# One bank for the small results of logits, routing and slots, the experts' order copied by VectorE, and one conversion step moved

## The chip, the core and the metric

The kernel runs on one core of a Trainium2 chip. The metric is the device time of one execution in microseconds (us), median of three runs. The core has five engines with an instruction queue each, which run in order: TensorE (PE; its weight loads are shown as PEld), VectorE (DVE), ScalarE (ACT), GpSimd (POOL) and SyncE (SP), which only issues transfers here. PE writes its results to PSUM, eight banks of 512 float32 columns in 128 partitions.

## What is computed

Two batches of 768 tokens pass through three layers: attention over a window with a few global keys, a mixture of experts with one expert for each token, and a mixing layer.

```python
scores = q @ k.T / 8 - slopes * dist          # 8 heads of 64, window of 96, 8 global keys
attn = softmax(where(keep, scores, -1e9)) @ v
logits = x @ w_gate                           # 8 experts
local = sigmoid(x @ w_local)
e[s] = argmax(logits[s]) if s == 0 or local[s] < 0.5 else e[s - 1]
out[s] = softmax(logits[s])[e] * (relu(x[s] @ w1[e]) @ w2[e])
theta = out @ w_theta
y = w_tok_r @ (out * cos(theta)) + w_tok_i @ (out * sin(theta))
u = out + y
result = u + relu(u @ w_ch)
```

## The kernel before

The order of all instructions is written out by hand; the framework adds the waits on semaphores. The work falls into attention with routing, the experts and the mixing layer. This change lies in the first of them and in its passage to the second.

**The attention loop.** There are 12 blocks of 128 tokens, each with 4 units (a unit is two heads). The loop over `s` has 24 steps of two units each, so a block takes an even and an odd step. Names of the pieces of work, as the list `TAIL` and the calls of `at` use them:

- `qk` scores on PE (L557); `sa`, `sb` the softmax of the two heads: a subtraction of the minimum on DVE (L579) and the exponential on ACT (L589).
- `tr` transposes the probabilities of a unit on PE into a tile `pt` (L612); `cp` copies it out, on ACT (L621) or, for every fourth unit, on DVE (L619); `pv` multiplies with the values (L636).
- For a block `i`: `ev` copies the result out (ACT, L648), `ri` takes the reciprocals (DVE, L602 and L603), `yt` transposes it on PE (L653) into a `pt` buffer, `ys` scales and stores it (DVE, L662; for the last two blocks ACT and POOL).
- The block's logits: `lg` on PE (L219), `lc` copies them on ACT (L223), `lt` transposes them on PE (L226), `ld` divides and sums on DVE (L231 writes `lh`, L237).
- Routing of a pair `t` of blocks: `ch` (DVE, L252 to L260), `ro` (PE, L266 and L267), `sc` (DVE, L272 and L274), `oh` (PE, L285), `ho` (DVE, L290), `po` (PE, L301 and L302), `pl` (DVE, L307 to L313), `mk` (POOL or DVE, L321), `sl` (PE, L330), `tk` (DVE, L341 and L343).
- `ha`, `hb`, `hr`, `ya`, `yb`, `px`, `pc`: an expert's first 128 tokens, computed ahead, on PE and ACT.
- `rk`, `en`: the experts' ranking and `experts_slots` on DVE. `le`, `lx`, `ls`: the choice of the expert that is computed ahead.
- `job_tick` (and `jt`): the next of six stages that convert a 512-column piece of a later layer's weights, on ACT and DVE; the fifth also issues the load of a later piece, the sixth is a subtraction on DVE (L414). `JATT` lists the steps that end with such a stage.

In the odd steps that end a pair, with X = 4t + 9, the order is `qk`, `oh`, `lc`, `lt`, `ys`, then the softmax of the first unit, `ho`, `ld`, then `tr`, `tr`. In the steps X = 4t + 11 `lc`, `lt`, `ys`, `ld`, `ch` come in the same places and `sl` ends the step. In the even steps `ro` or `po` follow `qk`, and `yt`, `lg` end the step.

**PSUM.** The pool `pT` has two buffers of one bank, tag `pt`, taken in turn. They hold the transposed probabilities, the transposed blocks (`yt`), the logits and the slots. The pool `pM` has one bank, tag `m`, which holds the routing's small results (`misc`) and the warm-up's. The choice between the two:

```python
def mps(own):
    return (pM if own else pT).tile([128, 512], F32, tag="m" if own else "pt", name="m")
```

**The passage to the experts.** SP loads the weights in pieces. The first load of `w1` needs `first_i` only; every later one needs `order_g`, a copy of `order_i` that POOL makes behind three gathers of tokens (L1029, L1040). The first piece's `w2` (L1017), the next pieces and all that follow stand behind that.

Of the kernel before, what the change touches and what calls it, by code (L numbers as in the profile page):

```python
# [9 lines left out]
F32 = mybir.dt.float32  # L10
F32R = mybir.dt.float32r
BF16 = mybir.dt.bfloat16
I32 = mybir.dt.int32
AF = mybir.ActivationFunctionType
# [42 lines left out]

TAIL = """
ev10 ro4 tk3 tr46 tr47 sc4 cp46 oh4 ho4 cp47 pv44 pv45 yt10 lg10 ri10 lc10 po4 pl4 px pc lt10 ys10 ld10 pv46 pv47 ev11
ri11 mk4 ha0 hb0 hr0 jt yt11 lg11 lc11 jt ha1 hb1 hr1 lt11 ld11 ys11 sl4 tk4 ya0 yb0 ch5 ha2 hb2 hr2 ro5 sc5 ya1 yb1 oh5  # L60
jt ho5 ha3 hb3 hr3 po5 pl5 ya2 yb2 mk5 rk ha4 hb4 hr4 sl5 tk5 ya3 yb3 ha5 hb5 hr5 en ya4 yb4 ha6 hb6 hr6 ya5 yb5 ha7 hb7
hr7 ya6 yb6 ya7 yb7 ye
"""
# [4 lines left out]
CPV0 = (1, 3)  # L68


JATT = (4, 5, 6, 8, 9, 10, 12, 13, 14, 16, 17, 18, 20, 21, 22)
JRATE = (0.8, 1.4, 1.3, 1.9, 2.5, 2.5, 1.6)
T1, T2, T3 = 2, 2, 2
JBUFS = 3
# [26 lines left out]
def kernel(  # L101
# [13 lines left out]
    V, A, G, PE, SP = nc.vector, nc.scalar, nc.gpsimd, nc.tensor, nc.sync  # L115
# [6 lines left out]
    def ct(shape, dt, name):  # L122
        return const.tile(shape, dt, name=name, tag=name)
# [9 lines left out]
    wg = ct([128, 4, 32], F32, "wg")  # L133


    ident = ct([128, 128], F32, "ident")
# [73 lines left out]
    def logit_stages(blk, xT, rinv, ps, sb):  # L210

        st = {}

        def logits():

            lp = ps(False)[:, 0:256].rearrange("p (i c) -> p i c", i=2)
            lT = sb([128, 128], "lT")
            for j in range(4):
                PE.matmul(lp[32 * j : 32 * j + 32, 0], lhsT=wg[:, j], rhs=xT[:, j], start=True, stop=True)  # L219
            st["lT"], st["lp"] = lT, lp  # L220

        def logits_copy():
            A.activation(st["lT"], st["lp"][:, 0], AF.Copy)  # L223

        def total_tr():
            PE.transpose(st["lp"][:, 1], st["lT"], ident)  # L226

        def total():
            lp = st["lp"]
            lh = sb([128, H, 9], "lh")  # L230
            V.tensor_tensor(  # L231
                lh.rearrange("p (j w) e -> p j w e", w=2),
                lp[:, 1].rearrange("p (j c) -> p j c", j=4)[:, :, 0:18].rearrange("p j (w e) -> p j w e", w=2),
                rinv.rearrange("p (j w) -> p j w", w=2).unsqueeze(3).to_broadcast([128, 4, 2, 9]),
                op=ALU.mult,
            )
            V.tensor_reduce(Lall[:, blk], lh.rearrange("p h e -> p e h"), axis=AX.X, op=ALU.add)  # L237

        return [logits, logits_copy, total_tr, total]

    def route_stages(t, ps, sb, slots=True):

        st = {}
# [18 lines left out]

        def rows():
            cb = st["cb"]
            misc = st["ps"] = ps(True)
            PE.matmul(misc[0:B, 0:128], lhsT=cb[:, 0], rhs=identb, start=True, stop=True)  # L266
            PE.matmul(misc[0:B, 128:256], lhsT=cb[:, 1], rhs=identb, start=True, stop=True)  # L267

# [53 lines left out]

        def slot():
            if slots:
                tk = st["tk"] = ps(False)[:, 0:64].rearrange("p (i w e) -> p i w e", i=4, w=2)
                n = width // 128
                for i in range(n + 1):
                    ohs = [x[:, i * 128 : min(i * 128 + 128, width)] for x in st["ohl"]]
                    for b in range(B):
                        PE.matmul(  # L330
                            tk[: ohs[b].shape[1], i],
                            lhsT=ohs[b],
                            rhs=st["bm"][:, :, b],
                            start=(b == 0),
                            stop=(b == B - 1),
                        )
# [44 lines left out]
    def job_load():  # L381
        k = jstate["loaded"]
        if k < len(jobs):
            t = jpool[0].tile([128, 512, 2], I32, tag="jraw", name="jraw", bufs=jstate["bufs"])
            W = 512 // len(jobs[k][0])
            for i, src in enumerate(jobs[k][0]):
                jstate["eng"].dma_start(
                    t[:, i * W : i * W + W], src.bitcast(I32).rearrange("p (c w) -> p c w", w=2)
                )
            jraw[k] = t  # L390
            jstate["loaded"] = k + 1
# [24 lines left out]
    def job_tick(n=1):  # L416
        for _ in range(n):
            if jstate["gen"] is None:
                if jstate["k"] not in jraw:
                    return  # L420
                jstate["gen"] = job(jstate["k"])
                jstate["k"] += 1
            if next(jstate["gen"], 0) == 0:
                jstate["gen"] = None
# [3 lines left out]
            job_tick()  # L428
    order_i = ct([1, 8], I32, "order_i")
    first_i = ct([1, 1], I32, "first_i")  # L430
    flag_i = ct([1, 1], I32, "flag_i")
    xall = ct([128, 25], I32, "xall")
    xidx = xall[:, 0:24].rearrange("p (r i) -> p r i", i=3)
# [11 lines left out]
    with ExitStack() as actx:  # L445
# [3 lines left out]
        pT = actx.enter_context(tc.tile_pool(name="pT", bufs=2, space=PSUM))  # L449
        pX = actx.enter_context(tc.tile_pool(name="pX", bufs=1, space=PSUM))  # L450
        pM = actx.enter_context(tc.tile_pool(name="pM", bufs=1, space=PSUM))
# [26 lines left out]
        wm = ap.tile([128, 512], BF16, tag="wm", name="wm", bufs=1)  # L478
# [189 lines left out]
            i = BLOCKS.index(n)  # L668
            SP.dma_start(xd[i * 128 : (i + 1) * 128, :], xt)

        def mps(own):
            return (pM if own else pT).tile([128, 512], F32, tag="m" if own else "pt", name="m")

        def msb(shape, name, dt=F32):
            return ap.tile(shape, dt, tag=name, name=name, bufs=2)
# [137 lines left out]
        def experts_slots():  # L813
# [37 lines left out]
            V.tensor_reduce(ordf[:, 0, 0:1], over, axis=AX.X, op=ALU.max)  # L851
            V.tensor_tensor(flag_i, ordf[:, 0, 0:1], ordf[:, 1, 0:1], op=ALU.max)

        pairs, later = {}, {}

        def warm(k):

            if k:
                w = pM.tile([128, 512], F32, tag="m", name="warm")
            for _ in range(k):  # L860
                PE.matmul(w, lhsT=wm[:, 0:128], rhs=wm, start=True, stop=True)

        def fill():
            if "zero" not in head:
# [57 lines left out]


        warm(NWARM)
        biases(0, 0)
        biases(0, 1)
# [4 lines left out]
        for s in range(NS):  # L931
# [18 lines left out]
            if s >= 2:  # L950
                run(f"pv{u - 4} pv{u - 3}")
                if s % 2:
                    i, t = s // 2 - 1, (s // 2 - 1) // B
# [20 lines left out]
            if s in (1, 2):  # L974
                job_load()
            if s in JATT:
                job_tick()
# [58 lines left out]
    load_piece(0, (1,))  # L1036
    for n in range(1, 4):
        gather_x(n)
    order_g = ct([1, 8], I32, "order_g")
    G.tensor_copy(order_g, order_i)  # L1040


    ptok = ct([128, NB], F32, "ptok")
# [22 lines left out]
    def general():  # L1066
        with ExitStack() as gctx:
            xTd = dram.tile([NB, 128, 512], F32, name="xTd", tag="xTd")
            with ExitStack() as c1:
                g1 = c1.enter_context(tc.tile_pool(name="g1", bufs=1, side="right"))  # L1070
                p1 = c1.enter_context(tc.tile_pool(name="p1", bufs=1, space=PSUM))

                def gps(own):
                    return p1.tile([128, 512], F32, tag="x", name="gm")

                def gsb(shape, name, dt=F32):
                    return g1.tile(shape, dt, tag="g" + name, name="g" + name, bufs=2 if shape[-1] <= 128 else 1)
# [3 lines left out]
                for b in range(B):  # L1081
                    for t in range(NT):
# [22 lines left out]
                        V.tensor_tensor(il, il, rel, op=ALU.mult)  # L1105
                        V.tensor_tensor(kd, kd, il, op=ALU.add)
                        V.tensor_scalar(rel, kp, NEG, -NEG, op0=ALU.mult, op1=ALU.add)
                        xp = gps(True).rearrange("p (j c) -> p j c", j=4)
                        for h in range(H):
                            j, hh = divmod(h, 2)  # L1110
                            if hh == 0:
                                k_s, vb = [g1.tile([128, NT, 128], F32, tag=n, name=n) for n in ("gk", "gv")]
                                c = slice(j * 288 + 160, j * 288 + 288)
                                SP.dma_start(k_s, pack[b, :, :, c].rearrange("t p c -> p t c"))
                                c = slice(1664 + j * 128, 1792 + j * 128)
# [3 lines left out]
                            st = gsb([128, 2], "st")  # L1119
                            for c in range(2):  # L1120
# [3 lines left out]
                                    lhsT=q_s[p0 : p0 + 64, j * 128 : (j + 1) * 128],  # L1124
                                    rhs=k_s[p0 : p0 + 64, 3 * c : 3 * c + 3],
                                    start=True,
                                    stop=True,
# [16 lines left out]
                            pt = [gsb([128, 3, 128], f"pt{c}") for c in range(2)]  # L1144
# [6 lines left out]
                            for c in range(NT):  # L1151
                                PE.matmul(
                                    xp[p0 : p0 + 64, j],
                                    lhsT=vb[:, c, p0 : p0 + 64],
                                    rhs=pt[c // 3][:, c % 3],
                                    start=(c == 0),
                                    stop=(c == NT - 1),
                                )
                        blk = b * NT + t
                        xT = g1.tile([128, 4, 128], F32, tag="gxT", name="gxT")  # L1160
# [7 lines left out]
            with ExitStack() as c2:  # L1168
# [3 lines left out]
                for g in range(4):  # L1172
                    xT = g2.tile([128, 3, 4, 128], F32, tag="xT", name="gxT")
# [5 lines left out]
                    for e in range(E):  # L1179
                        yp = [p2.tile([128, DM], F32, tag=f"y{i}", name="gyp", bufs=1) for i in range(3)]  # L1180
                        for n in range(4):
                            a = g2.tile([128, 4, 256], F32, tag="w1", name="gw1")
                            c = g2.tile([128, 2, DM], F32, tag="w2", name="gw2")
# [4 lines left out]
                            for f in range(2):  # L1188
                                hp = p2.tile([128, 3, 128], F32, tag="h", name="ghp")
                                for j in range(4):  # L1190
                                    PE.matmul(
                                        hp,
                                        lhsT=a[:, j, f * 128 : (f + 1) * 128],
                                        rhs=xT[:, :, j],
                                        start=(j == 0),
                                        stop=(j == 3),
                                    )
                                V.tensor_scalar(hs[:, f], hp, 0.0, None, op0=ALU.max)
                                for i in range(3):
                                    PE.matmul(  # L1200
                                        yp[i],
                                        lhsT=hs[:, f, i],
                                        rhs=c[:, f],
                                        start=(n == 0 and f == 0),
                                        stop=(n == 3 and f == 1),
                                    )
                        for i in range(3):
                            k = 3 * g + i
# [3 lines left out]
                    for i in range(3):  # L1212
                        k = 3 * g + i
# [157 lines left out]
    with ExitStack() as mctx:  # L1371
# [260 lines left out]
        for u in range(64):  # L1632
# [77 lines left out]
            i = f - (1 if r else GP)  # L1710
# [12 lines left out]
            i = f - (2 if r else XF)  # L1723
# [377 lines left out]
```

## Time and profile before

| | us |
|---|---|
| median of 3 runs (481.68 to 481.9) | 481.73 |
| the profiled execution | 481.55 |
| its span, first to last instruction | 476.0 |
| PE busy | 464.5 (98%) |
| DVE busy | 348.9 (73%) |
| ACT busy | 256.4 (54%) |
| POOL busy | 138.8 (29%) |

The span is counted from the first instruction. "Idle before" and the name in brackets behind an instruction say how long its engine stood idle ahead of it and what released it, by the semaphores. Ends of matmuls are modelled, so a busy PE is not PE at its peak. The granted clock of PE was 0.998 over the span.

### The profile page before, as it was taken

What the parts mean: (1) busy time and instruction counts of PE and PEld (TensorE: products, weight loads), DVE (VectorE), ACT (ScalarE), POOL (GpSimd) and SP (SyncE); (2) the same over time, 40 slices, a digit from 0 to 9 for tenths busy, and PEclk for the clock granted to TensorE, in tenths of its full rate; (3) what the DMA queues carried; (4) which work ended last, traced back from release to release, by engine and by line L of the source; (5) the groups of instructions that cost most, each with busy time, mean ns of one, the idle gap of its engine ahead of it and who ended that gap; (6) DMA issues with size and microseconds to landing.
All of it is one profiled execution on the core that took longest, in us unless ns stands there. A gap on an engine that the chain in (4) does not pass through costs nothing.

```text
span 476.0 us, 9458 instructions
## 1 busy us (share of the span) xinstructions
PE 464.5 (98%) x3311; PEld 382.6 (80%) x3311; DVE 348.9 (73%) x916; ACT 256.4 (54%) x615; POOL 138.8 (29%) x188
## 2 busy tenths in 40 slices
PE   8999998999999999999999999999999999999995
PEld 4677776778888898888887778888888888888885
DVE  5888878867687788877687676576999899751422
ACT  5978786832455666665555564455655355520300
POOL 8502213224122404040513032203454332430400
PEclk9999999999999999999999999999999999999999
DMA  8978577623966798887999993600022100001022
GB/s 234 365 214 275 179 235 233 234 90 96 352 191 195 272 290 264 289 265 247 295 303 330 305 299 131 205 23 22 23 67 92 43 21 22 1 33 35 33 80 91
DMA packets 60410, 82.97 MB, mean 174 GB/s; under 512 B 5528, under 2 KB 39576, under 8 KB 60360
## 3 DMA queue, kind: packets, MB, share of 16 engines
q1 hardware_dynamic: 52500, 62.65, 40.2%
q0 software_dynamic: 4272, 9.92, 6.7%
q10 hardware_dynamic: 3588, 9.77, 6.3%
q8 instruction: 27, 0.44, 0.4%
q14 instruction: 23, 0.19, 0.1%
HBM read 70.94 MB, written 11.38 MB: 173 GB/s over the span
## 4 chain that ended last, share of the span: by engine, by line
PE 74%; DVE 8%; DMA 8%; issue 4%; ACT 4%; POOL 2%; ACTq 0%; SPq 0%; DVEq 0%; POOLq 0%
PE a L1860 21%; PE o L1549 9%; PE b L1897 7%; PE h L1493 7%; PE th L1784 7%; PE h L1476 4%; PE x L636 3%; PE s L557 3%; DMA raw<-in_w_dram 3%; PE pt L612 3%; DMA yd<-yo 3%; DVE sm L579 2%; ACT pr L589 2%; PE o L1565 2%; DMA ps<-pd,toks 1%
## 5 line engine op out<-in xcount | busy, mean ns | idle before, releaser
L1860 PE MATMUL a<-wtokr,z 128*128 128x512 f32 x480 | 85.9, 337 | 0.0
L1860 PEld LDWEIGHTS a<-wtokr,z 128*128 128x128 f32 x480 | 73.8, 188 | 9.3
L1549 PE MATMUL o<-w2s,hh 128*128 128x512 f32 x192 | 62.9, 407 | 0.4 <-DVE w2s L1458 0.3
L589 ACT ACTIVATE pr<-sm,st 128x256 f32<-128x256 f32 (+1 forms) x96 | 46.0, 482 | 16.7 <-DVE st L579 16.5
L1493 PE MATMUL h<-xT,w1s 128*128 128x288 f32 (+3 forms) x384 | 51.8, 284 | 0.9 <-DVE xT L1331 0.5
L1493 PEld LDWEIGHTS h<-xT,w1s 128*128 128x128 f32 x384 | 48.7, 189 | 4.0 <-DVE w1s L1354 0.9
L1458 DVE TENSOR_TENSOR w2s<-raw,w2s 128x512 fp32r<-128x512 f32 x56 | 38.4, 686 | 15.7 <-ACT w2s L1457 15.7
L579 DVE CUSTOM_DVE_ANT_0 sm<-s,bias 128x256 f32<-128x256 f32 (+1 forms) x96 | 33.9, 394 | 11.7 <-PE s L557 10.3
L1476 PEld LDWEIGHTS h<-xT,raw 128*128 128x128 f32 x256 | 37.0, 190 | 4.4 <-issue 3.9
L1476 PE MATMUL h<-xT,raw 128*128 128x192 f32 (+3 forms) x256 | 40.5, 311 | 0.0
L1457 ACT ACTIVATE w2s<-raw 128x512 fp32r<-128x512 f32 x56 | 35.0, 627 | 8.2 <-PE o L1549 4.0
L1549 PE MATMUL o<-w2s,hl 128*128 128x512 f32 x96 | 37.9, 395 | 0.5 <-DVE hl L1524 0.5
L1549 PEld LDWEIGHTS o<-w2s,hh 128*128 128x128 f32 x192 | 32.3, 184 | 6.6 <-DVE w2s L1458 1.4
L1601 POOL DMA_DIRECT2D yd<-yo x13 | 8.3, 637 | 81.4 <-ACT yo L1599 81.4
L1905 DVE SCALAR_TENSOR_TENSOR ob<-b,xTf 128x512 f32<-128x512 f32 (+1 forms) x16 | 8.8, 556 | 27.2 <-PE b L1897 27.1
L1816 POOL TENSOR_TENSOR si<-si,yg 128x512 f32<-128x512 f32 x10 | 13.5, 1345 | 51.0 <-ACT si L1809 48.1
L1354 DVE TENSOR_TENSOR w1s<-raw,w1s 128x512 fp32r<-128x512 f32 x32 | 21.9, 688 | 8.1 <-ACT w1s L1353 7.6
L612 PE MATMUL pt<-ident,pr 128*128 128x128 f32 x176 | 26.1, 281 | 1.8 <-DVE lh L231 0.7
L557 PE MATMUL s<-kall,q 64*128 64x256 f32 (+1 forms) x192 | 26.2, 391 | 0.0
L411 ACT ACTIVATE wtokr<-jw 128x512 fp32r<-128x512 f32 x15 | 9.5, 632 | 29.6 <-DVE jw L408 29.6
L404 DVE SCALAR_TENSOR_TENSOR jw<-jraw,jw 128x512 int32<-128x512 int32 x26 | 24.7, 952 | 0.4
L406 DVE SCALAR_TENSOR_TENSOR jw<-jraw,jw 128x512 int32<-128x512 int32 x26 | 24.6, 945 | 0.1
(292 smaller groups left out, 975.1 us busy)
## 6 DMA issues: line engine op xcount, KB each, us to landing
raw<-in_w_dram SPq DMA_DIRECT2D x60, 512.0 KB, 5.4
vv<-in_pack_dram SPq DMA_DIRECT2D x10, 512.0 KB, 5.6
jraw<-in_w_tokT_dram ACTq DMA_DIRECT2D x10, 512.0 KB, 4.5
w<-in_w_dram SPq DMA_DIRECT2D x16, 256.0 KB, 5.7
kall<-in_pack_dram SPq DMA_DIRECT2D x10, 320.0 KB, 3.7
xd<-xt SPq DMA_DIRECT2D x12, 256.0 KB, 3.7
q<-in_pack_dram SPq DMA_DIRECT2D x11, 256.0 KB, 4.1
jraw<-in_w_tokT_dram ACTq DMA_DIRECT2D x10, 256.0 KB, 4.4
```

The lines of the kernel that those rows point to most:

```text
L557: PE.matmul(sp[hh][:, 0:W], lhsT=qs[n][half, j], rhs=kall[half, b, j, t * 160 + 160 - W : t * 160 + 160], start=True, stop=True,)
L579: V.tensor_tensor_reduce(out=sm[:, hh, 0:W], in0=ust[u]["s"][hh], in1=bias[:, 2 * j + hh], scale=-0.125, scalar=BIG, op0=ALU.add, op1=ALU.min,
L589: A.activation(pr[:, hh, 0:W], sm[:, hh, 0:W], AF.Exp, bias=st[:, hh : hh + 1], scale=-1.0, accum_out=sums[n][:, 2 * j + hh : 2 * j + hh + 1],
L612: PE.transpose(pt[:, hh, c], pr[:, hh, c * 128 : (c + 1) * 128], ident)
L1457: A.activation(h2, bb[:, o], AF.Copy)
L1458: V.tensor_tensor(l2, bb[:, o], f32(h2), op=ALU.subtract)
L1476: PE.matmul(hp[:, :N], lhsT=pieces[u // 2][1][:, j, o * 128 : (o + 1) * 128], rhs=x[:, j, :N], start=(j == 0), stop=(j == 3),)
L1493: PE.matmul(hp[:, :N], lhsT=wa[:, j], rhs=xa[:, j, :N], start=(k == 0), stop=(k == 11))
L1549: PE.matmul(out[:M], lhsT=ha[:, lo : lo + M], rhs=wa, start=(f == 0 and q == 0), stop=(f == 7 and q == 2),)
L1784: PE.matmul(th, lhsT=xa[:, j], rhs=wa[:, j], start=(n == 0), stop=(n == 11))
L1860: PE.matmul(acc[b][d][o], lhsT=za[:, d * 128 : (d + 1) * 128], rhs=wa[:, lo:hi], start=(t == 0 and n == 0 and (o == 0 or d % 2 == 0)), sto ...
L1897: PE.matmul(op[:, : hi - lo], lhsT=wa[:, d, e * 128 : (e + 1) * 128], rhs=ua[d][:, lo:hi], start=(n == 0), stop=(n == 11),)
```

## The change

- `small`, one tile in `pM`, is made once and kept. The routing's results keep columns 0 to 304 of it, logits and their transpose both take columns 304 to 432, the slots 432 to 496. `pT` is left to the transposed probabilities and blocks.
- The warm-up writes to `small` too.
- The copy of the experts' order becomes the last instruction of `experts_slots`, on DVE; POOL's copy is gone.
- In `TAIL`, `ya0 yb0` move ahead of `sl4`, and `ch5` ahead of `tk4`.
- The conversion stage of step 18 moves to step 19.

The branch `general()`, where `gps` loses its argument, isn't taken with these inputs.

```diff
-ri11 mk4 ha0 hb0 hr0 jt yt11 lg11 lc11 jt ha1 hb1 hr1 lt11 ld11 ys11 sl4 tk4 ya0 yb0 ch5 ha2 hb2 hr2 ro5 sc5 ya1 yb1 oh5
+ri11 mk4 ha0 hb0 hr0 jt yt11 lg11 lc11 jt ha1 hb1 hr1 lt11 ld11 ys11 ya0 yb0 sl4 ch5 tk4 ha2 hb2 hr2 ro5 sc5 ya1 yb1 oh5
...
-JATT = (4, 5, 6, 8, 9, 10, 12, 13, 14, 16, 17, 18, 20, 21, 22)
+JATT = (4, 5, 6, 8, 9, 10, 12, 13, 14, 16, 17, 19, 20, 21, 22)
...
         def logits():
-            lp = ps(False)[:, 0:256].rearrange("p (i c) -> p i c", i=2)
+            lp = ps()[:, 304:432]
...
-                PE.matmul(lp[32 * j : 32 * j + 32, 0], lhsT=wg[:, j], rhs=xT[:, j], start=True, stop=True)
+                PE.matmul(lp[32 * j : 32 * j + 32], lhsT=wg[:, j], rhs=xT[:, j], start=True, stop=True)
...
-            A.activation(st["lT"], st["lp"][:, 0], AF.Copy)
+            A.activation(st["lT"], st["lp"], AF.Copy)
...
-            PE.transpose(st["lp"][:, 1], st["lT"], ident)
+            PE.transpose(st["lp"], st["lT"], ident)
...
-            misc = st["ps"] = ps(True)
+            misc = st["ps"] = ps()
...
-                tk = st["tk"] = ps(False)[:, 0:64].rearrange("p (i w e) -> p i w e", i=4, w=2)
+                tk = st["tk"] = ps()[:, 432:496].rearrange("p (i w e) -> p i w e", i=4, w=2)
...
-        def mps(own):
-            return (pM if own else pT).tile([128, 512], F32, tag="m" if own else "pt", name="m")
+        small = pM.tile([128, 512], F32, tag="m", name="small")
+
+        def mps():
+            return small
...
             V.tensor_tensor(flag_i, ordf[:, 0, 0:1], ordf[:, 1, 0:1], op=ALU.max)
+            V.tensor_copy(order_g, order_i)
...
         def warm(k):
-            if k:
-                w = pM.tile([128, 512], F32, tag="m", name="warm")
             for _ in range(k):
-                PE.matmul(w, lhsT=wm[:, 0:128], rhs=wm, start=True, stop=True)
+                PE.matmul(small, lhsT=wm[:, 0:128], rhs=wm, start=True, stop=True)
...
-    order_g = ct([1, 8], I32, "order_g")
-    G.tensor_copy(order_g, order_i)
```

## Rows read from the trace of the kernel before

**Rows 1.** Windows: stretch, length, busy time of each engine, clock, DMA, GB/s.

```profile
70.00:80.00 10.00, 9.32 (x101) 6.58 (x101) 8.59 (x48) 7.68 (x26) 3.45 (x5) 1.00 0.69 223
130.00:140.00 10.00, 10.00 (x76) 8.81 (x75) 8.68 (x29) 5.89 (x13) 1.59 (x2) 1.00 0.70 221
```

**Rows 2.** Chain of waits, passage to the experts: start, length, what.

```profile
116.14 0.65 POOL order_g L1040
...
117.77 4.29 DMA raw<-in_w_dram
122.07 0.64 ACT w2s L1457
122.80 0.70 DVE w2s L1458
```

**Rows 3.** Timeline, passage: start, length, engine, line, operation, tiles, count, idle before.

```profile
112.90 0.16 DVE L831 CAST order_i<-ordf 1x8 int32<-1x8 f32 x1
...
115.41 0.15 DVE L852 TENSOR_TENSOR flag_i<-ordf 1x1 int32<-1x1 f32 x1
...
121.23 0.38 ACT L1528 ACTIVATE hh<-h 128x256 fp32r<-128x256 f32 x1 [1.83 <-PE h L1493]
```

**Rows 4.** Timeline, step 17, logits and routing.

```profile
64.66 0.28 ACT L223 ACTIVATE lT<-m 128x128 f32<-128x128 f32 x1 [0.65 <-PE m L219]
...
65.58 0.39 PE L285 MATMUL m<-own,erow 2*128 2x16 f32 x2
...
65.91 0.33 PE L226 MATMUL m<-ident,lT 128*128 128x128 f32 x1
...
66.08 0.17 DVE L290 TENSOR_TENSOR ohb<-m,rev 128x16 bf16<-128x16 f32 x1
```

**Rows 5.** Timeline, tail, block 10 and pair 4.

```profile
97.64 0.18 PE L301 MATMUL m<-ohb,ones 128*128 128x16 bf16 x1
...
97.68 0.17 PE L302 MATMUL m<-ohb,upper 128*128 128x16 bf16 x1
...
97.77 0.28 ACT L223 ACTIVATE lT<-m 128x128 f32<-128x128 f32 x1 [2.10 <-PE m L219]
97.89 0.17 DVE L307 TENSOR_TENSOR cum<-m,cum 128x8 f32<-128x8 f32 x1 [0.82 <-PE m L302]
...
98.18 0.27 PE L226 MATMUL m<-ident,lT 128*128 128x128 f32 x1
98.18 0.15 DVE L309 TENSOR_TENSOR cum<-m,cum 128x8 f32<-128x8 f32 x1
```

**Rows 6.** Timeline, transposes of steps 9, 11 and 19, and step 18's end.

```profile
33.54 1.14 PE L612 MATMUL pt<-ident,pr 128*128 128x128 f32 x8
...
41.91 0.66 PE L612 MATMUL pt<-ident,pr 128*128 128x128 f32 x4 [0.17 <-DVE lh L231]
...
72.94 0.64 DVE L414 TENSOR_TENSOR wtok<-jw,wtok 128x512 fp32r<-128x512 f32 x1
...
74.23 0.66 PE L612 MATMUL pt<-ident,pr 128*128 128x128 f32 x4 [0.51 <-DVE xt L662]
...
77.78 0.42 DVE L579 CUSTOM_DVE_ANT_0 sm<-s,bias 128x256 f32<-128x256 f32 x1 [0.89 <-PE s L557]
```

**Rows 7.** Timeline, step 20.

```profile
78.31 1.20 PE L612 MATMUL pt<-ident,pr 128*128 128x128 f32 x8
...
81.66 0.43 PE L219 MATMUL m<-xT,wg 128*32 128x128 f32 x8 [0.53 <-DVE ps L619]
```

**Rows 8.** Timeline, waits of PE in the tail.

```profile
94.36 1.06 PE L612 MATMUL pt<-ident,pr 128*128 128x128 f32 x8 [0.38 <-DVE toks L343]
...
102.88 0.40 PE L330 MATMUL m<-rbm,ohl 128*128 128x16 bf16 x6 [0.33 <-DVE lh L231]
```

**Rows 9.** Timeline, tail, POOL's multiply and `ch5` on DVE.

```profile
103.32 1.04 POOL L662 TENSOR_TENSOR xt<-xt,sums 128x512 f32<-128x512 f32 x1 [2.74 <-ACT xt L660]
...
103.58 0.81 DVE L256 TENSOR_SCALAR rcb<-Lall 128x2 bf16<-128x2 f32 x1
```

## What I expect of the change, and why

> **What bounds the kernel now.** I read the windows first. In the attention stretch TensorE (PE) is nearly full but not quite: 9.32 of 10 us between 70 and 80 us, with VectorE (DVE) at 8.59; in the experts after 130 us PE is full [rows 1]. A microsecond lost or won on PE before 130 us should therefore arrive at the end one for one, and one won on any other engine arrives only where PE was waiting for that engine. The chain of waits names one place where a copy decides: the experts' order is copied on GpSimd (POOL) at 116.14, the first load that needs it is issued by SyncE (SP) at 117.77 and lands 4.29 us later, ScalarE (ACT) and DVE split it, and the second half is there for PE at 122.80+0.70 = 123.50 [rows 2]. The timeline then shows which small waits of PE come from the two banks of the transposed probabilities (below). Steps are the 24 passes of the loop over `s`; their names are in the list of the kernel above.
>
> **The waits that the change removes.** Logits and slots no longer take one of the two `pt` buffers. Before, a block's rotation is tr, tr, yt, lg; in the odd step after it the first transposes wait for `ys`, the second for `ld`. After, it is tr, tr, yt; the first then wait for a copy of the step before, long done, the second only for `ys`.
> - Steps 11, 15, 23: eight transposes without a wait take 1.14 us; in step 11 four run, 0.17 idle for `lh`, four more in 0.66: 0.66+0.17+0.66 = 1.49, so 0.35 each [rows 6]. Steps 15 and 23 show the same pattern. In step 23 it is not kept: the next PE work, `ro4`, needs DVE's `ch4`. So -0.70.
> - Step 19: 0.51 for `xt` [rows 6], which stands behind the job's subtraction of 0.64 on DVE, plus the same 0.35: -0.86. The change also moves this subtraction from the end of step 18 to the end of step 19. It is the sixth and last stage of the job: it issues one DVE instruction and no DMA (the load is issued in the fifth), so no queue of SP or POOL is touched. Its cover there is DVE's 0.89 us idle ahead of step 20's softmax [rows 6], enough for 0.64; without that cover it would delay step 20 by 0.64.
> - Step 20: `lg` waits 0.53 for DVE's copy `ps` [rows 7]. It now shares no buffer with that copy: -0.53.
> - Steps 12, 16, 20: the second transposes wait for `tk`; eight take 1.20 instead of 1.14 [rows 6, 7]: -0.06 x 3 = -0.18.
>
> **The waits that it adds.** All small results now lie in one tile, `small`, one bank. The rows show how the program guards a bank: `cum` (L307) reads only what L301 wrote (columns 288 to 304), yet is released by L302, which wrote columns 272 to 288 [rows 5]. So a reader waits for every earlier write to its tile, whichever columns, and a writer for every earlier reader. I read off what the program order makes of that.
> - Steps 9, 13, 17, 21 run `oh`, `lc`, `lt`, `ho`, `ld`. Before, ACT's `lc` ran beside the scores, at 64.66, and `lt` followed `oh` on PE at once, at 65.91 [rows 4]. Now `lc` must wait for `oh`, which ends at 65.58+0.39 = 65.97. ACT follows PE by 0.06, copies in 0.28, and PE starts `lt` 0.13 after the copy (97.77+0.28 = 98.05 to 98.18) [rows 5]: `lt` at 65.97+0.06+0.28+0.13 = 66.44, that is +0.53. Queued behind it on PE are the step's transposes and everything after; behind `lc` on ACT the exponentials; on DVE `ho` now waits for `lt`'s end. DVE idles before the following scores, so I put these under PE's delay. Bounds: 0 (no wait) to 0.73 (DVE's delay, 66.44+0.33+0.04 against 66.08 as DVE's first instruction after `oh` now). I take 0.53, from the rows of the same hand-over: 4 x 0.53 = +2.12.
> - Sum up to the tail: 2.12-0.70-0.86-0.53-0.18 = -0.15.
> - Tail, block 10: `tr46` no longer waits 0.38 for `tk3` [rows 8]; `oh4` then waits for the scan and keeps about 0.25 of it. But `po4`, which ran with `lg10` at 97.64, now waits for `lc10`; and `lt10`, behind the lead's transposes, waits for `pl4`, whose last read of the bank starts 0.29 after its first and ends 0.15 later (97.89 to 98.18+0.15) [rows 5]. Shifting by the 0.25: `lc10` ends 97.80, `po4` 97.93 to 98.15, `pl4` 98.19 to 98.63, `lt10` 98.70 against 98.18: +0.52.
> - Tail, block 11: `sl4` waited 0.33 for `lh` [rows 8]; with `ya0 yb0` moved ahead, PE works on while DVE reads, and this is gone: -0.33. `ch5` moves ahead of `tk4`; but `ro5` writes the bank and must wait for `tk4`'s two adds too. Before, one instruction of `ch5` took 0.81, until POOL's multiply ended at 103.32+1.04 = 104.36 [rows 9]. If one of `ch5` is caught again, `ch5` ends as before and `tk4` follows it (0.2 an estimate, two adds of the kind of the cast's 0.16 [rows 3], overlapped): `ro5` +0.20 instead of -0.33. If none is, PE sets `ro5`: -0.33. Which of them is caught after the move no row shows; I take the middle, -0.07.
>
> The Trainium skill (SBUF — State Buffer, Who interferes with whom) says that a DVE instruction with two SBUF inputs contends with a GpSimd instruction that reads SBUF, and that whoever issues first holds the shared ports for the whole instruction. L256, held up in the row, has one such input; the two after it (L258) have two. By that rule the wait would only move from L256 to L258, and the sum below would be +0.12, 481.9.
>
> - Experts' order: on DVE the copy costs what the cast of the same eight numbers costs, 0.16 [rows 3], instead of POOL's 0.64 behind three gathers. The last instruction of `experts_slots` ends at 115.41+0.15 = 115.56, the new copy behind it at 115.7, POOL's at 116.14+0.65 = 116.79: the loads are issued 1.08 earlier. Of that the start of the second products gets less: ACT's `w2s` stands in order behind the first relu, which waits for PE and ends at 121.23+0.38 = 121.61 [rows 3], so it starts 0.46 earlier than 122.07 [rows 2], and DVE's part, for which PE waits, 0.45 earlier: -0.45. Late next is the first relu. DVE's next instructions are pushed by 0.16 under its wait for PE's transposes. POOL's next gather waits for PE anyway.
>
> **The sum.** -0.15+0.52-0.07-0.45 = -0.15 us. The profiled execution took 481.55 (476.0 of it the span, 5.55 around it); that makes 481.4. The median of the three runs, 481.73, is 0.18 above it: 481.6. The ends of the unknown costs: 0 to 0.73 for the bank wait (-2.12 to +0.80) and -0.33 to +0.20 at `ro5`. A measurement of this kernel can tell about 0.2%, 1 us, from no change.
>
> **Rivals.**
> - *The shared bank costs nothing*: waits go by columns, not by bank, and the change is only the removal of waits. Then +2.12 falls away, and of the tail's +0.52 also the 0.25 that `tr46` won counts, 0.77: -0.15-2.12-0.77 = -3.0, 478.7. For it: nothing depends by data. Against it: the releaser of L307 [rows 5]. The Trainium skill (PSUM — Partial Sum Buffer, PSUM bank collisions raise a hardware error) asks for guarding by bank and quadrant, not by address; by that rule this rival falls.
> - *Slower: DVE is what ends last.* `ho` sits in DVE's queue ahead of `ld` and two softmax passes; where its wait for `lt` counts, each of the four steps costs 0.73 and not 0.53 (+0.80), and the transposes that no longer wait for `lh` wait as long for `ys`, which stands only two softmax passes ahead of it on the same queue, so 0.70, 0.35 of step 19 and 0.18 do not come (+1.23). -0.15+2.03 = +1.9, 483.6. It decides once DVE reaches `ys` more than 0.6 us later than now. For it: DVE at 8.59 of 10; against: DVE idles for the scores in every even step (0.89 in the row).
> - *The loads pay in full*: all 1.08 of the earlier loads reach PE, if the relu is not in the way: -0.15-0.63 = -0.8, 480.9.
>
> **How the numbers follow.** Forecast 0.58 (481.6; faster 0.13, same 0.40, slower 0.05, as the bounds of the bank wait and of `ro5` put about a fifth of it beyond 1 us on the fast side and a tenth on the slow one); no bank wait 0.12 (all faster); DVE last 0.18 (slower 0.15, same 0.03); loads in full 0.12 (faster 0.05, same 0.07). Together faster 0.30, same 0.50, slower 0.20. The range leaves out the first rival and the far half of the second: 480.0 to 483.3.
>
> **What would show it.** In steps 9, 13, 17 and 21 `lT` (L223) starts right after `oh` (L285) and PE idles about 0.5 ahead of L226; if L223 still runs beside the scores, the first rival is right. PE's waits for `lh` and `toks` ahead of `pt` are gone; if as long ones for `xt` stand there, the second. The chain no longer names POOL's `order_g`, and the first load of `w2` is issued near 116.7. A start of that load near 117.7, or an end of the attention over 1 us away from now, makes the prediction wrong.

## The result, and the profile after

| | before | after |
|---|---|---|
| median of 5 executions, us | 481.8 (481.68 to 482.25) | 477.33 (476.16 to 478.38) |
| ratio | 1 | 0.9909 (95% interval 0.9888 to 0.9929) |
| the profiled execution | 481.55 | 478.38 |
| its span | 476.0 | 476.6 |
| around the span | 5.55 | 1.78 |

The change makes the kernel faster by 0.9%. The forecast was 481.6 with a range from 480.0 to 483.3 and "no change" as the likeliest case: it was wrong. The last two lines of the table hold the first surprise: in the two profiled executions the span did not get shorter at all. The gain of 3.17 stands outside it (5.55 became 1.78), in the time that the prediction carried over as a constant.

What stands there can be read in the view of the DMA transfers, asked for the time behind the last instruction. Kernel before, 476 to 484 us (the GB/s line has 40 slices of 0.2 us; below it queue and kind, packets, MB, share of 16 engines):

```profile
GB/s 0 0 0 0 0 0 0 0 0 0 0 0 0 82 82 82 0 0 0 0 0 0 0 0 0 0 0 0 0 0 0 0 0 0 0 0 0 0 0 0
DMA packets 5, 0.05 MB, mean 6 GB/s; under 512 B 0, under 2 KB 0, under 8 KB 0
...
q14 instruction: 4, 0.03, 1.5%
q8 instruction: 1, 0.02, 0.8%
```

The same view of the changed kernel, 477 to 485 us:

```profile
DMA packets 0, 0.00 MB, mean 0 GB/s; under 512 B 0, under 2 KB 0, under 8 KB 0
```

Before, five blocks of instructions are loaded from 2.8 us behind the last instruction of the kernel on (slices 13 to 15: 478.6 to 479.2), and the execution's end comes after them. After, nothing is loaded there.

Inside the span the view by stretches answers [rows 1]: PE went from 9.32 to 9.85 of the 10 us between 70 and 80, so waits of PE did disappear.

```profile
70.00:80.00 10.00, 9.85 (x116) 7.32 (x115) 9.41 (x51) 7.69 (x27) 4.23 (x5) 1.00 0.68 219
130.00:140.00 10.00, 10.00 (x76) 8.67 (x75) 8.73 (x30) 5.32 (x12) 2.04 (x2) 1.00 0.52 159
```

Taken from the starts of each step's first scores (L557, now L558), and counted from step 4 on, the changed kernel reaches the transposes of the experts' rows 1.13 earlier. Two further profiles of the two kernels give 1.12, and repeat each step's length to 0.02. An end of the attention over 1 us away was one of the signs that the prediction had named against itself. Step by step, in us, beside what the prediction had:

| steps | predicted | measured |
|---|---|---|
| 4 to 8 | 0 | -0.20 |
| 9, 13, 17, 21 (`oh lc lt`) | 4 x 0.53 = +2.12 | 4 x 0.33 = +1.31 |
| 10, 14, 18, 22 | 0 | +0.09, 0.00, +0.16, +0.25 = +0.50 |
| 11, 15, 19 | -0.35, -0.35, -0.86 = -1.56 | -0.50, -0.53, -1.12 = -2.15 |
| 12, 16, 20 | -0.06, -0.06, -0.59 = -0.71 | -0.11, -0.11, -0.71 = -0.93 |
| 23, tail, lead | +0.52 - 0.07 = +0.45 | +0.33 |
| together | +0.30 | -1.13 (terms rounded) |

From the passage to the end of the span, two profiles of the changed kernel differ by 1.2 us and two of the kernel before by 2.6, so what is left there is told from medians of many executions, below.

The rows behind the table. Timeline of the changed kernel, step 17, which answers [rows 4]:

```profile
64.95 0.39 PE L285 MATMUL small<-own,erow 2*128 2x16 f32 x2
...
65.38 0.28 ACT L223 ACTIVATE lT<-small 128x128 f32<-128x128 f32 x1 [1.64 <-PE small L285]
...
65.71 0.33 PE L226 MATMUL small<-ident,lT 128*128 128x128 f32 x1 [0.37 <-ACT lT L223]
```

The copy `lT` now starts 0.04 behind `oh` (64.95+0.39 = 65.34) and names it as its releaser, though `oh` writes other columns: the bank is guarded as a whole, as predicted. From the start of `oh` to that of `lt` it takes 0.76 instead of 0.33.

Transposes of steps 11 and 19, which answer [rows 6], and the first product behind each:

```profile
41.32 1.04 PE L613 MATMUL pt<-ident,pr 128*128 128x128 f32 x8
42.29 0.44 PE L637 MATMUL x<-ps,vv 128*64 128x128 f32 x4
```

```profile
73.42 1.04 PE L613 MATMUL pt<-ident,pr 128*128 128x128 f32 x8
74.39 0.44 PE L637 MATMUL x<-ps,vv 128*64 128x128 f32 x4
```

The waits for `lh` and `xt` are gone, eight transposes stand in one piece, and the products start 0.97 behind their first. Step 18's end and step 20's logits (the second answers [rows 7]):

```profile
71.25 0.66 PE L654 MATMUL y<-ident,xT 128*128 128x128 f32 x4 [0.15 <-ACT ps L622]
```

```profile
79.69 0.43 PE L219 MATMUL small<-xT,wg 128*32 128x128 f32 x8
```

The logits wait for nothing any more; but `yt` (L654) now waits 0.15 for ACT's copy `ps`, a wait that the prediction did not have.

The tail, which answers [rows 5, 8, 9]:

```profile
96.28 0.17 PE L301 MATMUL small<-ohb,ones 128*128 128x16 bf16 x1 [0.39 <-ACT lT L223]
...
97.08 0.14 PEld L226 LDWEIGHTS small<-ident,lT 128*128 128x128 f32 x1 [0.36 <-DVE cum L309]
...
102.22 0.39 PE L330 MATMUL small<-rbm,ohl 128*128 128x16 bf16 x6
102.22 0.16 DVE L256 TENSOR_SCALAR rcb<-Lall 128x2 bf16<-128x2 f32 x1
102.28 1.04 POOL L663 TENSOR_TENSOR xt<-xt,sums 128x512 f32<-128x512 f32 x1 [3.08 <-ACT xt L661]
102.34 1.15 DVE L258 SCALAR_TENSOR_TENSOR rval<-Lall,mxall,rev 128x8 f32<-128x8 f32 x2
```

Of the kernel before, the instructions that follow on [rows 9]:

```profile
104.31 0.35 DVE L258 SCALAR_TENSOR_TENSOR rval<-Lall,mxall,rev 128x8 f32<-128x8 f32 x2
```

In the changed kernel `po4` waits for `lc10`, `lt10` waits for the last read of `pl4`, `sl4` waits for nothing: all three as predicted. And the passage, which answers [rows 2, 3]:

```profile
114.34 0.15 DVE L856 TENSOR_TENSOR flag_i<-ordf 1x1 int32<-1x1 f32 x1
114.42 0.15 DVE L858 COPY order_g<-order_i 1x8 int32<-1x8 int32 x1
115.80 0.40 SPq L1021 DMA_DIRECT2D raw<-in_w_dram  x1
...
120.39 0.38 ACT L1530 ACTIVATE hh<-h 128x256 fp32r<-128x256 f32 x1 [1.81 <-PE h L1495]
120.67 0.62 ACT L1459 ACTIVATE w2s<-raw 128x512 fp32r<-128x512 f32 x1
121.38 0.69 DVE L1460 TENSOR_TENSOR w2s<-raw,w2s 128x512 fp32r<-128x512 f32 x1
```

### The profile page after: what moved, and what is told of

The parts are those of the page before. It is cut to its first block, busy times and chain, and to the rows that moved or that the text cites. A ratio compares the mean times of both kernels' runs of the same rounds, so it can differ in the third digit from the quotient of the medians.

```text
span 476.6 us, 9463 instructions
## 1 busy us (share of the span) xinstructions
PE 462.0 (97%) x3311; PEld 382.3 (80%) x3311; DVE 349.1 (73%) x917; ACT 255.3 (54%) x615; POOL 137.2 (29%) x187
## 4 chain that ended last, share of the span: by engine, by line
PE 65%; DVE 10%; issue 8%; ACT 7%; DMA 5%; POOL 2%; ACTq 1%; SPq 0%; DVEq 0%; POOLq 0%
PE a L1862 21%; PE b L1899 7%; PE th L1786 7%; PE o L1551 6%; PE h L1495 5%; PE s L558 4%; PE x L637 3%; DMA yd<-yo 3%; PE pt L613 3%; DVE w2s L1460 2%; ACT pr L590 2%; PE h L1478 2%; PE y L654 1%; DVE jw L406 1%; POOL xg L1033 1%
## 5 line engine op out<-in xcount | busy, mean ns | idle before, releaser
L558 PE MATMUL s<-kall,q 64*128 64x256 f32 (+1 forms) x192 | 25.5, 384 | 1.5 <-DMA kall<-in_pack_dram 1.4
L637 PE MATMUL x<-ps,vv 128*64 128x128 f32 x352 | 24.5, 279 | 0.0
```

Of the source, the lines that this page charges most:

```text
L558: PE.matmul(sp[hh][:, 0:W], lhsT=qs[n][half, j], rhs=kall[half, b, j, t * 160 + 160 - W : t * 160 + 160], start=True, stop=True,)
L637: PE.matmul(xp[64 * hh : 64 * hh + 64, j], lhsT=vv[:, i, h * 64 : (h + 1) * 64], rhs=ps[:, hh, c], start=(c == 0), stop=(c == nch - 1),)
```

## The experiments

Two theories on the first surprise stood against each other at first: the gain comes from the shared bank inside the span, or from what GpSimd's copy does to the time around it. Every run has 10 executions of its kernel. They were taken in three groups of four runs, in the order of the table, each group beside 30 or 31 executions of the kernel before on the same chip; every execution has its own span. "GpSimd rows" counts the instructions of GpSimd in the profile, its waits on semaphores included. "With loads" counts the executions with 4.6 to 6.1 around the span; the others have 1.75 to 1.96, and nothing lies between. This is inferred from the time: of each kernel one execution was kept as a profile. Every profile with over 4.6 shows the five blocks behind its end, every one with under 2 none.

| run | GpSimd rows | span, median | with loads | time, median | ratio to before (95%) |
|---|---|---|---|---|---|
| before, beside the three groups | 281 | 477.0 | 70 of 92 | 482.2, 481.1, 482.0 | |
| b_again | 281 | 477.6 | 8 of 10 | 482.39 | 0.9956 to 1.0025 |
| bank_only | 281 | 475.8 | 9 of 10 | 480.77 | 0.9954 to 1.0023 |
| order_only | 280 | 477.2 | 0 | 479.05 | 0.9919 to 0.9971 |
| a_again | 280 | 475.6 | 0 | 477.33 | 0.9891 to 0.9947 |
| pool_copy | 282 | 476.0 | 10 | 481.68 | 0.9984 to 1.0054 |
| pool_memset | 281 | 475.8 | 7 | 480.71 | 0.9933 to 1.0012 |
| other_moved | 280 | 476.9 | 0 | 478.67 | 0.9928 to 0.9986 |
| no_copy | 280 | 481.3 | 0 | 483.13 | 1.0004 to 1.0073 |
| lc_first | 280 | 474.6 | 0 | 476.49 | 0.9877 to 0.9940 |
| order_late | 280 | 477.1 | 0 | 479.00 | 0.9924 to 0.9999 |
| pool_two | 282 | 475.7 | 10 | 481.35 | 0.9965 to 1.0029 |
| both | 280 | 478.0 | 0 | 479.72 | 0.9940 to 1.0008 |

**b_again, a_again**: the two kernels, unchanged.

> The kernel before, unchanged, to see how its time and its span stand to each other in several executions. If what lies around the span (5.55 us in the profiled execution before, 1.78 after) belongs to the program, the time is 481.7 +- 0.3 and the span 476.0 +- 0.7 in each, 5.5 apart. If it only belongs to one execution, the distance varies from execution to execution, between 1.8 and 5.6.

> The changed kernel, unchanged. If what lies around the span belongs to the program: 477.3 +- 1.2, span 474.3 to 476.6, 1.8 apart in each. If it belongs to the execution, some of them show 5.5 and a time near 481.

Measured: in the kernel before it belongs to the execution: 4.6 to 5.8 around the span in eight, 1.8 in two. In the changed kernel it is 1.75 to 1.93 in all ten, as the first time. Its span is 1.5 shorter than the 477.1 of the kernel before beside it. That b_again, the same kernel, has 477.6 shows that a median of ten spans can be off by 0.5.

**bank_only**: the kernel before, with the shared bank alone (lines of the logits and the warm-up that are not shown are those of the change).

```diff
-            lp = ps(False)[:, 0:256].rearrange("p (i c) -> p i c", i=2)
+            lp = ps()[:, 304:432]
...
-                tk = st["tk"] = ps(False)[:, 0:64].rearrange(...)
+                tk = st["tk"] = ps()[:, 432:496].rearrange(...)
...
+        small = pM.tile([128, 512], F32, tag="m", name="small")
```

> The kernel before with the shared bank alone; the order of the experts stays with POOL, the hand-written order and the conversion step stay. By the sum of the prediction without its last terms (no subtraction moved, no POOL copy moved): span within 1 us of the kernel before. If the shared bank is what takes the 3.8 us from around the span: 478 with 1.8 around the span. If it isn't: 481.5 to 482.5 with 5.5 around it.

Measured: span 1.3 shorter, the time around it as before. In its profile the passage comes 0.77 earlier than in that of b_again; all steps up to 18 are those of the changed kernel. The missing 0.35 belongs to the moved conversion: step 19 gains 0.88 instead of 1.12, step 20 0.61 instead of 0.71. From step 22 to the passage it loses 0.60 and the changed kernel 0.58, so the reordered tail gained next to nothing there.

**order_only**: the kernel before, with the order copied by VectorE alone.

```diff
+            V.tensor_copy(order_g, order_i)
...
-    G.tensor_copy(order_g, order_i)
```

> The kernel before with the experts' order copied by VectorE alone. By the sum: span shorter by 0.45, time 481.3 if what lies around the span stays at 5.5. If the missing POOL copy is what takes 3.8 us from around the span: 477.5 with 1.8 around it.

Measured: the span is that of before, and in all ten executions only 1.77 to 1.89 are left around it. So the two parts are independent: the bank shortens the span, the copy's move takes away the loads behind the end. The next three runs ask what in the copy brings them.

**pool_copy, pool_memset, pool_two**: the changed kernel, with one line (pool_two: two) added behind the three gathers.

```diff
+    G.tensor_copy(e0_i, order_i[:, 0:2])     (pool_copy)
+    G.memset(e0_i, 0)                        (pool_memset, pool_two)
+    G.memset(e0_i, 1)                        (pool_two)
```

> The changed kernel, and one GpSimd copy of two integers of the order (into e0_i, dead by then) back at the place where the order's copy stood, behind the three gathers; nobody waits for it. The order that the loads read is still VectorE's. Theory 1 (one more instruction in GpSimd's program adds the 3.3 us around the span, whatever it does): span as the changed kernel's, 475.5, and about 5 around it instead of 1.8: 480.5. Theory 2 (it is this kind of instruction, GpSimd's copy of integers): also 480.5. Theory 3 (SyncE's wait for GpSimd's copy is what adds it): 477.3, nothing changes.

> As the run before, with a GpSimd fill of the same two integers instead of the copy. Theory 1 (any GpSimd instruction more): 480.5, about 5 around the span. Theory 2 (this kind of copy) and theory 3 (SyncE's wait): 477.3, 1.8 around it.

**other_moved**: the kernel before; its copy of the order stays on GpSimd, another instruction leaves it.

```diff
-        G.memset(cum[:, 0], 0.0)
+        V.memset(cum[:, 0], 0.0)
```

> The kernel before, with another instruction moved from GpSimd to VectorE: the fill of cum's first column with zeros, among the constants at the start. The order's copy stays on GpSimd and SyncE waits for it. Theory 1 (one GpSimd instruction less): about 1.8 around the span instead of 5, span as before's 477.2: 479.0. Theories 2 and 3 (the copy itself, or the wait for it): 482.2, nothing changes.

Measured: theory 1 in all three. GpSimd's rows are 282 in pool_copy, since the copy brings a wait on a semaphore as a row of its own, and 281 in pool_memset. A fill that nobody waits for brings the loads back (7 of 10), and moving a fill at the program's start takes them away while the copy stays where it was. Transfers of pool_memset, 477 to 484 us, and of other_moved in the same stretch:

```profile
DMA packets 5, 0.05 MB, mean 7 GB/s; under 512 B 0, under 2 KB 0, under 8 KB 0
...
q14 instruction: 4, 0.03, 1.6%
q8 instruction: 1, 0.02, 0.9%
```

```profile
DMA packets 0, 0.00 MB, mean 0 GB/s; under 512 B 0, under 2 KB 0, under 8 KB 0
```

> The changed kernel with two more GpSimd fills of e0_i (282 GpSimd rows; before has 281, changed has 280). If the instructions loaded behind the end come with a length of GpSimd's program above some bound between 280 and 281: about 5 around the span, 480.7. If they come with an odd number of instructions, or with the alignment of one instruction: 1.8 around it, 477.3.

Measured: 282 rows, loads in 10 of 10. It is not an odd number that counts. With 280 rows (75 executions, the changed kernel's first five among them) the loads never come, with 281 in 94 of 122, with 282 in 20 of 20.

**no_copy**: the changed kernel without a second tile; SyncE reads `order_i`.

```diff
-            V.tensor_copy(order_g, order_i)
...
-            regs[k] = SP.value_load(order_g[0:1, r : r + 1] ...
+            regs[k] = SP.value_load(order_i[0:1, r : r + 1] ...
```

> The changed kernel without any copy of the order: SyncE reads order_i itself. One VectorE instruction less, GpSimd as changed. Theory 1 and 2: 477.3 less at most the 0.16 of the copy inside the span, 1.8 around it. If what counts is that VectorE's program got longer by one, the 3.3 come back: 480.5.

Measured: no loads behind the end, but the span is 5.7 longer than the changed kernel's. Timeline of no_copy at the passage:

```profile
113.42 0.38 SPq L1019 DMA_DIRECT2D raw<-in_w_dram  x1
...
115.68 0.28 ACT L775 ACTIVATE lead_r<-h 128x128 f32<-128x128 f32 x1 [2.78 <-PE h L770]
...
118.19 0.63 PE L1325 MATMUL tr<-ident,xg 128*128 128x128 f32 x4 [0.62 <-DMA xg<-xd,xall]
...
120.20 0.43 PE L1325 MATMUL tr<-ident,xg 32*128 32x32 f32 x4 [1.37 <-DMA xg<-xd,xall]
```

The loads are issued 2.25 earlier than in the profile of a_again (115.67), and a relu of the lead that needs none of them starts 1.31 later than there (114.37), though PE wrote its last input at the same time. Then PE's transposes wait 0.62 and 1.37 for the gathered rows `xg`; in a_again all twelve run in one piece (1.66). By the first of the second products (L1549) no_copy is 3.07 behind a_again, and it loses the rest later.

**order_late**: as no_copy, but the copy that writes `order_i` stands behind the other steps of `experts_slots`, so that the loads are issued as late as in the changed kernel.

```diff
-            V.tensor_copy(order_i, ordf[:, 0])
             V.tensor_tensor(over, ordf[:, 1], capr, op=ALU.is_gt)
...
+            V.tensor_copy(order_i, ordf[:, 0])
             V.tensor_reduce(ordf[:, 0, 0:1], over, axis=AX.X, op=ALU.max)
```

> The changed kernel without the second tile: SyncE reads order_i itself, as in the run without a copy, but the one copy that writes it stands near the end of experts_slots, not in the middle. The run without a copy had a span 5.8 longer, and its first loads were issued 2.2 earlier than the changed kernel's. If the early loads are what cost it (they fill the DMA engines ahead of the gathers of the experts' rows), they are issued here some 0.25 earlier than in the changed kernel and the span is within 0.5 of its 475.5: 477.3. If reading order_i itself costs it (another release of SyncE, another place of the tiles), the span stays near 481 and the time near 483.

Measured: span 477.1, with a spread from 476.0 to 479.9. Neither expectation held: 4.2 of the 5.7 are gone with the early loads, 1.5 are not. In its profile the first of the second products starts earlier than in a_again (its weight load 107.89 against 108.15 behind step 4's start), so the loss comes later. Its three longest spans (478.9 to 479.9) have a mean granted clock of 0.994 or 0.995, the other seven (476.0 to 477.9) 0.997 to 1.0. So early loads cost most of the 5.7, a part of the rest goes with the clock, and what brings that stays open.

**lc_first**: the changed kernel with `lc lt` ahead of `oh`.

```diff
-                    at(s + 2, 0, f"lc{i} lt{i} ys{i}")
+                    later[s + 2, 0] = f"lc{i} lt{i} " + later.get((s + 2, 0), "") + f" ys{i}"
```

> The changed kernel, with lc and lt put ahead of oh in the odd steps (in steps 9, 13, 17 and 21 they stood behind it). In the profile of the changed kernel each of these four steps is 0.33 longer than before. If that is PE's wait for a copy that the shared bank holds up behind oh, lc runs beside the scores again, lt and oh follow on PE without a wait, and the four steps give back 0.33 each: span 475.5 - 1.3 = 474.2, time 476.0. If VectorE is what ends last in these steps, the wait moves to the transposes or to the second scores and nothing is won: 477.3; if oh, now later on PE, holds up ho on VectorE, 478.

Measured: steps 9, 13 and 17 each take 3.69 instead of 3.98, as the theory has it. Step 21 takes 4.28. Its timeline, step 17 first:

```profile
63.42 0.14 PEld L226 LDWEIGHTS small<-ident,lT 128*128 128x128 f32 x1 [0.33 <-issue]
...
63.68 0.39 PE L285 MATMUL small<-own,erow 2*128 2x16 f32 x2
```

```profile
79.80 0.33 PE L226 MATMUL small<-ident,lT 128*128 128x128 f32 x1 [0.52 <-ACT lT L223]
80.05 0.39 PE L285 MATMUL small<-own,erow 2*128 2x16 f32 x2
```

In step 21 ACT is late with `lT` (it runs at 79.47, behind a conversion stage of 0.66 that ACT begins at 78.92), and now `oh` stands behind it too. Together 0.68 at the passage, and 1.0 in the median span: 474.6. With 476.5 against 477.3 this is the fastest kernel here, though the intervals of the two overlap.

**both**: lc_first and order_late together.

> lc_first and order_late together, without the additional fills. If the two theories on them hold: span 474.2, 1.8 around it, 476.0, faster than both kernels. If neither holds: 483.

Measured: span 478.0. The gain of lc_first is there up to the passage: 0.68, as in lc_first. It is lost right behind it. Timeline of both, and the view by stretches:

```profile
115.65 0.63 PE L1325 MATMUL tr<-ident,xg 128*128 128x128 f32 x4 [0.26 <-DMA xg<-xd,xall]
116.93 0.43 PE L1325 MATMUL tr<-ident,xg 32*128 32x32 f32 x4 [0.65 <-DMA xg<-xd,xall]
```

```profile
116.00:118.00 2.00, 0.87 (x8) 0.55 (x7) 0.72 (x3) 1.11 (x2) 1.57 (x2) 1.00 0.88 317
118.00:120.00 2.00, 2.00 (x10) 2.00 (x10) 1.68 (x4) 0.00 (x0) 0.95 (x1) 0.50 1.03 350
120.00:122.00 2.00, 2.00 (x12) 2.00 (x12) 0.57 (x3) 0.90 (x2) 0.00 (x0) 0.65 1.07 375
```

PE waits for gathered rows again and is busy for 0.87 of 2 us; then its granted clock is 0.50, the lower of its two levels, for 3.4 us (from 118.0 on; 0.65 is the mean of the last stretch). The second products begin 7.83 behind the first transpose, in lc_first 5.86. In the profile of no_copy PE stood idle there as well and the clock stayed at 1.00, so the clock is no sure price of such waits.

## Why the prediction was wrong, point by point

**The step that failed first** is the one before the sum: "481.55 (476.0 of it the span, 5.55 around it)". The 5.55 was added back as a constant. It is one of two values: in the 92 executions of the kernel before, 70 have a median of 5.34 around the span, 22 of 1.85. The edit that changes it was in the prediction, but with its price inside the span alone (-0.45). order_only shows the rest: about 3.4 in three of four executions. The view that would have shown that something is there is the one of the transfers behind the last instruction, and the prediction did not read it. That one GpSimd instruction less would remove it could not be read from the trace of before.

**The shared bank is guarded as a whole**: right. `lT` names `oh`, `po4` waits for `lc10`, `lt10` for `pl4`. The rival without a bank wait fell.

**Its price of 0.53** was too high; measured 0.33 a step, so 0.8 too much over four. Between `oh` and `lt` it is 0.43, because PE follows ACT's copy by 0.05 (65.38+0.28 to 65.71), not by the 0.13 that I took from a row of the tail. Another 0.1 comes back at once: the products start 0.96 behind the first transpose, before 1.08.

**The waits removed** were priced too low: -0.50, -0.53 and -1.12 where the sum had -0.35, -0.35 and -0.86. I compared the length of a group, 1.14, with the broken one, 1.49. What a step pays is from start to start, and unhindered that is 0.97, as PE's next work overlaps the end of the last transpose. The same effect gave -0.24 and -0.21 in steps 5 and 7, which the prediction did not have at all; step 6 gives 0.24 back (its transposes last 1.24 instead of 1.09, and `yt` waits 0.26 for `ps` instead of 0.17).

**A wait not seen**: `yt` for ACT's `ps` in steps 10, 18 and 22 (0.15 in the row of step 18). lc_first, which lets `lc` run beside the scores again, takes 4.22 and 4.12 in steps 18 and 22 instead of 4.32 and 4.34 (before 4.16 and 4.10).

**Step 20's logits and the moved subtraction** were right in size: -0.71 for -0.59; DVE's idle time ahead of step 20 covered the subtraction.

**The tail**: +0.33 for +0.45. Of block 11 I had taken the middle between "one instruction of `ch5` is caught" and "none is". One is caught: L256 runs in 0.16, and one of the two L258 lasts until GpSimd's multiply ends (102.28+1.04 = 103.32); the two take 1.15, before 0.35. The Trainium skill (SBUF — State Buffer, Who interferes with whom) says that a DVE instruction with two SBUF inputs contends with a GpSimd instruction that reads SBUF; the trace agrees for L258, which has two. It does not show that the single input of L256 is what freed it: before, L256 began 0.26 behind the multiply's start and took 0.81 [rows 9], now it begins 0.06 ahead of it (102.22 and 102.28). bank_only, with the old order of the tail, loses as much from step 22 on, so the new order was worth next to nothing.

**The experts' order** on DVE: the loads are issued at 115.80, 0.91 earlier counted from the first experts' transposes, and DVE's `w2s` comes 0.35 earlier (5.40 behind the first of them, 5.75 before). That is near the -0.45. Little of it arrives: in order_only's profile the end of the first group of second products is 0.17 earlier by the same count, and its median span is that of before. The rival in which all 1.08 arrive falls, and in no_copy, with loads 2.25 earlier than in the changed kernel, the span is longer.

**DVE last**, the slower rival, did not come: the transposes of steps 11 and 19 wait for nothing.

So inside the span the mechanism was right in the main and its sizes were not: +0.30 at the passage against -1.13, and -1.5 in the medians of the spans. Of the 1.43 between the two sums, 0.81 is the bank's wait (+2.12 against +1.31), 0.81 the waits that fell away (-2.27 against -3.08), steps 4 to 8 and the tail 0.32 together, and the unseen wait of `yt` takes 0.50 back. The rest of the 4.8 between the medians, some 3.3, is the loads behind the end.

## What to carry to other kernels

Read the time around the span as a term of its own, with the transfers behind the last instruction, over several executions: where it takes two values, an edit that adds or removes a single instruction can decide between them, and here a copy, a fill behind it and a fill at the program's start did it alike. Cost a wait from start to start of the work on both sides of it, in a step that has the wait and in one that has not, not by the lengths of the groups. When results are packed into one guarded bank, look for the pairs of writer and reader that the program's order puts back to back, and swap them where the engine between them is free.

## What the runs showed of the hardware that was not expected

With 280, 281 and 282 rows on GpSimd the five blocks behind the end (four of 8 KB, one of 16 KB) were loaded in none, in 94 of 122 and in all executions, by the time around the span, and the time differs by about 3.4 us between executions of one kernel that load them and those that don't (before: 482.21 and 478.80, with a median span of 477.0 in both). VectorE's rows (1122 to 1135 in these kernels) do not decide it: the changed kernel and pool_memset both have 1135, without loads and with. The Trainium skill (Runtime: NRT & Kernel Launch, Instruction fetch mechanics) says that a taken branch to a block that isn't in the engine's window forces a load before the engine goes on. Whether the loads behind the end are of that kind no run here shows, nor which engine waits, why one row on GpSimd brings all five blocks, and what decides between two executions with 281.

Loads of weights issued 2.25 us earlier made the span 5.7 longer (no_copy). It began with ACT standing still for 1.31 us over an instruction whose inputs were there; what held it, the trace does not name. Then PE waited 1.99 us for gathered rows that came later than in a_again. How much of the rest is contention of transfers was not separated.
